# A fused convolution and two-layer network on Trainium2: weight conversion, first convolutions and first pairs in an interleaved order, part of the conversion on DVE

## The chip, the cores and the metric

The kernel runs on one core of a Trainium2 chip. The metric is the device time of one execution in microseconds. Times of one kernel are medians of several runs; a trace comes from one more execution, which has its own time.

## The reference

What is computed, cut to its core: a causal convolution of width 7, whose weights are a softmax for each token and head, and after it two matrix products with a leaky ReLU between them.

```python
# x: (4, 4096, 192), weight_gen: (4, 4096, 8, 7), w_in: (192, 2048), w_out: (2048, 192)
w = np.exp(weight_gen - np.max(weight_gen, axis=-1, keepdims=True))
w = w / (np.sum(w, axis=-1, keepdims=True) + 1e-09)
x_unf = x_pad[:, idx, :].reshape(B, S, K, H, group)      # the 7 last tokens of each token
x = np.einsum('bshk,bskhg->bshg', w, x_unf).reshape(B * S, D)
h = x @ w_in
g = np.maximum(0.01 * h, h)
return g @ w_out
```

The two weight matrices arrive as 64-bit numbers (two 32-bit words each). All results are 32-bit.

## The kernel before, in words

The 16384 tokens are cut into 32 chunks `c` of 512. The hidden layer's 2048 columns are cut into 8 pairs of 2 x 128, so there are 32 x 8 = 256 steps `q`, each with one chunk and one pair. `step(q)` issues `mm1` (18 matmuls into two PSUM buffers `hp`, tag `h`, of which there are four), then `act` for both (ACT applies the ReLU in place and makes the upper half `gh`; DVE subtracts and makes the lower half `gl`), and `mm2` for an earlier pair (20 matmuls into `po`). Every 32-bit operand is split into an upper and a lower half of the matmul's number format, and products are summed from the halves.

The weights are converted on the chip while the first chunk runs. There are 16 pieces: 8 of `w_in` (`wi_raw`, one for each pair) and 8 of `w_out` (`wo_raw`). Each goes through five stages, named by letters:

- `r`: ACT reads the low and the high words (L108, L109);
- `w`: DVE joins them in three instructions (L119, L121, L125), the first two in a PSUM buffer of tag `h`, and SP then gets the load of a later piece;
- `o`: an integer addition rounds up (L133), on POOL; the capital `O` does it on DVE;
- `u`: the upper half is cast (L154), on ACT; the capital `U` does it on DVE (L152);
- `l`: the lower half is subtracted (L158), on POOL; the capital `L` does it on DVE.

The convolution of chunk 0 (L246 and L256: three quarters of it on DVE, letters `d` and `e`; a quarter on POOL, letter `g`) ends in `twice` (L251), which PE transposes (`T`, L275). Chunk 1's convolution is POOL's (13 instructions, letter `p`). Its result is split (`c`: ACT L287; `v`: POOL L291), transposed in blocks by DVE (`t`, `m`: L297, into `sq`) and spread by 16 transfers of SP's queue into `xx` (`x`, L310). Step 8, the first step of chunk 1, needs these transfers. Later chunks go the same way, fed to the queues by `step` itself.

The order in which all this is handed out up to step 9 is the string `START`, one letter for one piece of work; `s` is one call of `step`. There is no scheduler: each engine runs what it is handed in that order, and waits where an operand or a buffer isn't ready. After the string, the remaining steps are handed out one after the other.

Of the kernel before, what the change touches and what calls it, by code (L numbers as in the profile page):

```python
# [24 lines left out]

C0 = 1

START = "ASrdegdegdegdegdegdegdegwOuLdegdegdegdegdegdegrTppppsrwoulppppsrwoulrwoulppppsrwoulrwoulpsrwoulrwoulcsrwoulrwoulvtsrwoulrwoulmxsrwoulrwoulsrwoulwoulss"


@with_exitstack
def conv_attention_moe_kernel(
# [390 lines left out]
    with tc.manual_schedule():  # L423
# [81 lines left out]
        n = 0  # L505
        for what in START:
            if what in stages:
# [62 lines left out]
```

## Time and profile before

| | |
|---|---|
| median of 3 runs | 1249.89 us (1249.32 to 1250.35) |
| the profiled execution's own time | 1249.38 us |
| its span in the trace | 1247.6 us |
| PE busy (matmuls) | 1164.3 us, 93% of the span |
| ACT busy | 885.0 us, 71% |
| POOL busy | 810.0 us, 65% |
| DVE busy | 598.5 us, 48% |
| mean granted TensorE clock | 0.97 |

Times in the trace are counted from the span's start. The execution's time is 1.8 us more than the span, and 0.5 us less than the median. Busy shares are means over the whole span; the first 203 us, in which the weights are converted and the first chunks are started, look different from the rest. Matmul ends are modelled, so a busy PE is read as "not waiting", not as PE at its peak.

### The profile page before, as it was taken

To read this page: it belongs to the slowest core of one execution; us is meant where nothing else is said; L and a number is where in the kernel's file an instruction comes from. 1 tells how busy PE (TensorE), PEld (TensorE's weight loads), DVE (VectorE), ACT (ScalarE), POOL (GpSimd) and SP (SyncE) were. 2 spreads that over 40 slices of the span, in tenths; PEclk is the share of its full clock that TensorE was granted. 3 is DMA by queue.
4 is the path that set the end of the run, shared out by engine and by line. 5 is a ranking of instruction groups with operands and counts; after the bars stand their busy time and mean duration, and the time that the engine had idled before them with its cause. 6 is when DMAs were issued, how large, how long until landed. Compare 5 with 4: busy or idle time off the path is not lost.

```text
span 1247.6 us, 24837 instructions
## 1 busy us (share of the span) xinstructions
PE 1164.3 (93%) x9740; PEld 989.1 (79%) x9740; DVE 598.5 (48%) x890; ACT 885.0 (71%) x1940; POOL 810.0 (65%) x535
## 2 busy tenths in 40 slices
PE   2567798999999999999999999999999999999997
PEld 1345676888888888888888888888888888888885
DVE  6345343544545444444545454544545444454443
ACT  2344664788777777878777777777777778877775
POOL 5845847777666667876666677766666677866400
PEclk9688988999999999999999999999999999999999
DMA  3424204242231324233231424223232424221220
GB/s 102 128 64 115 45 21 116 64 115 65 52 104 43 98 65 116 64 98 70 55 99 44 112 65 116 64 63 102 48 94 55 116 65 116 65 52 45 49 49 26
DMA packets 118306, 94.93 MB, mean 76 GB/s; under 512 B 9391, under 2 KB 111791, under 8 KB 116398
## 3 DMA queue, kind: packets, MB, share of 16 engines
q1 hardware_dynamic: 116110, 92.18, 29.1%
q10 hardware_dynamic: 2080, 1.18, 0.4%
q8 instruction: 76, 1.25, 0.4%
q14 instruction: 40, 0.33, 0.1%
HBM read 31.98 MB, written 12.58 MB: 36 GB/s over the span
## 4 chain that ended last, share of the span: by engine, by line
PE 89%; DVE 3%; ACT 2%; SPq 2%; POOL 1%; issue 1%; ACTq 1%; DMA 1%; DVEq 0%; POOLq 0%
PE po L357 46%; PE hp L329 43%; SPq L310 2%; ACT hp L336 1%; POOL bits L133 1%; ACTq L310 1%; ACT gh L338 0%; DVE gl L340 0%; DMA xx<-sq 0%; DVE h L246 0%; ACT wi_h L154 0%; DVE t L121 0%; DVE bits L125 0%; DVE sq L297 0%; POOL acc L256 0%
## 5 line engine op out<-in xcount | busy, mean ns | idle before, releaser
L329 PE MATMUL hp<-xx,wi_h 64*128 64x512 f32 x3072 | 583.2, 402 | 53.0 <-ACT wi_h L154 26.7
L340 DVE TENSOR_TENSOR gl<-hp,gh 128x512 fp32r<-128x512 f32 x512 | 353.4, 690 | 580.7 <-ACT gh L338 579.4
L357 PE MATMUL po<-gh,wo 64*128 64x512 f32 x3072 | 628.8, 393 | 0.0
L357 PE MATMUL po<-gl,wo 64*128 64x512 f32 x2048 | 547.9, 392 | 0.0
L329 PEld LDWEIGHTS hp<-xx,wi_h 64*128 64x128 f32 x3072 | 439.7, 189 | 111.0 <-ACT wi_h L154 36.4
L357 PEld LDWEIGHTS po<-gh,wo 64*128 64x128 f32 x3072 | 477.1, 185 | 51.8
L329 PE MATMUL hp<-xx,wi_l 64*128 64x512 f32 x1536 | 471.1, 401 | 0.1
L336 ACT ACTIVATE hp<-hp 128x512 f32<-128x512 f32 x512 | 299.9, 586 | 208.7 <-PE hp L329 208.7
L357 PEld LDWEIGHTS po<-gl,wo 64*128 64x128 f32 x2048 | 372.8, 184 | 34.2
L256 POOL TENSOR_TENSOR acc<-acc,tmp 128x768 f32<-128x768 f32 (+1 forms) x191 | 346.3, 1813 | 14.7
L338 ACT CAST gh<-hp 128x512 fp32r<-128x512 f32 x512 | 300.4, 587 | 16.2
L329 PEld LDWEIGHTS hp<-xx,wi_l 64*128 64x128 f32 x1536 | 283.1, 189 | 30.7 <-POOL wi_l L158 4.3
L246 POOL TENSOR_TENSOR tmp<-xt,wt 128x768 f32<-128x768 f32 (+1 forms) x192 | 291.4, 1518 | 12.5
L395 ACT COPY ot<-z 32x128 f32<-32x128 f32 x752 | 223.3, 297 | 11.6 <-DVE z L379 0.9
L291 POOL TENSOR_TENSOR split<-acc,split 128x768 fp32r<-128x768 f32 x31 | 57.5, 1854 | 184.6 <-ACT split L287 184.6
L370 ACT COPY sa<-po 128x512 f32<-128x512 f32 x64 | 37.5, 586 | 59.5 <-PE po L357 59.5
L209 POOL TENSOR_TENSOR wt<-wt,mx 128x448 f32<-128x448 f32 x15 | 14.6, 975 | 99.0 <-DVE mx L206 96.4
L371 DVE TENSOR_TENSOR sa<-po,sa 128x512 f32<-128x512 f32 x64 | 43.0, 672 | 45.5 <-ACT sa L370 45.5
L297 DVE STREAM_TRANSPOSE sq<-split 128x768 f32<-128x768 f32 x62 | 56.8, 953 | 0.0
L246 POOL TENSOR_TENSOR acc<-xt,wt 128x768 f32<-128x768 f32 (+1 forms) x32 | 48.9, 1528 | 0.1
L395 POOL COPY ot<-z 32x128 f32<-32x128 f32 x8 | 2.7, 332 | 62.0 <-DVE z L379 61.7
L133 POOL TENSOR_TENSOR bits<-bits,rnd 128x384 uint32<-128x384 uint32 x15 | 15.0, 997 | 27.3 <-DVE bits L125 27.3
(47 smaller groups left out, 265.4 us busy)
## 6 DMA issues: line engine op xcount, KB each, us to landing
xx<-sq SPq DMA_DIRECT2D x488, 96.0 KB, 2.3
xt<-in_x_dram SPq DMA_DIRECT2D x14, 1344.0 KB, 6.5
out_dram<-ot SPq DMA_DIRECT2D x32, 384.0 KB, 2.5
wt<-in_weight_gen_dram SPq DMA_DIRECT2D x16, 224.0 KB, 3.1
wo_raw<-in_moe_w_out_dram SPq DMA_DIRECT2D x8, 384.0 KB, 3.6
wi_raw<-in_moe_w_in_dram SPq DMA_DIRECT2D x14, 192.0 KB, 3.4
xt<-in_x_dram SPq DMA_DIRECT2D x1, 960.0 KB, 5.1
xx<-sq ACTq DMA_DIRECT2D x8, 96.0 KB, 3.9
```

Of the source, the lines that this page charges most:

```text
L246: eng.tensor_tensor(out=ov, in0=xv, in1=wk, op=ALU.mult)
L256: eng.tensor_tensor(out=acc, in0=acc, in1=out, op=ALU.add)
L291: eng.tensor_tensor(out=l, in0=att.pop(c), in1=h.bitcast(F32), op=ALU.subtract)
L297: nc.vector.transpose(out=sq[c][:, i], in_=split[c][:, i].bitcast(F32).rearrange("p j (b d) -> p b j d", d=BK),)
L329: nc.tensor.matmul(out=hp[2 * q + u], lhsT=w[s], rhs=r[s], start=(m == 0), stop=(m == len(passes) - 1),)
L336: nc.scalar.activation(out=t, in_=t, func=AF.Prelu, alpha=0.01)
L338: nc.scalar.copy(out=g_h[n], in_=t)
L340: nc.vector.tensor_tensor(out=g_l[n], in0=t, in1=g_h[n].bitcast(F32), op=ALU.subtract)
L357: nc.tensor.matmul(out=po[which, u], lhsT=wo[s, f, w], rhs=g[n][s], start=(f == 0 and m == 0), stop=(f == NF - 1 and m == len(passes) - 1),)
L370: nc.scalar.copy(out=a, in_=po[which, 0])
L371: nc.vector.tensor_tensor(out=a, in0=po[which, 1], in1=a, op=ALU.add)
L395: engs[n % len(engs)](out=ot[k * BK:(k + 1) * BK, :, a * BK:(a + 1) * BK], in_=src[:, k])
```

## The change

Only the string `START` is another one. The pieces of work are the same, with the same letters in another order; six of the 16 integer additions (`o`) have become `O` and run on DVE (one did before), five of the 16 lower halves (`l`) have become `L` (one before), and four of the 16 casts (`u`) have become `U` (none before).

```diff
-START = "ASrdegdegdegdegdegdegdegwOuLdegdegdegdegdegdegrTppppsrwoulppppsrwoulrwoulppppsrwoulrwoulpsrwoulrwoulcsrwoulrwoulvtsrwoulrwoulmxsrwoulrwoulsrwoulwoulss"
+START = "ASdeegdegddegddeeeeddegpggrgwgdgeOgdrepggeeduprgldpdwopTwurwpsLorwrpopurOulupplwsLwOprsOurlwpwuorsouurlwlOrwlurwlswprooucLouwtUvmosrLwrUlswoUOlxUlsLss"
```

How ACT's queue stands around the first step, before. The first row is the last ReLU of step 0, the last row the first one of step 1; `rnd` and `mag` are the low and the high words of a piece, `wi_h` is its upper half.

```order
L336 ACTIVATE hp<-hp 128x512
L338 CAST gh<-hp 128x512
L108 ACTIVATE rnd<-wi_raw 128x384
L109 ACTIVATE mag<-wi_raw 128x384
L154 CAST wi_h<-bits 128x3x128
L336 ACTIVATE hp<-hp 128x512
```

ACT's queue now, from the end of the first transposes (`xx<-ta`) to the first ReLU of step 0.

```order
L280 CAST xx<-ta 128x512 x3
L154 CAST wi_h<-bits 128x3x128
L108 ACTIVATE rnd<-wo_raw 128x384
L109 ACTIVATE mag<-wo_raw 128x384
L336 ACTIVATE hp<-hp 128x512
L338 CAST gh<-hp 128x512
```

The cast that step 1's `mm1` needs stood behind step 0's ReLUs and behind the reading of its own piece; now it stands ahead of step 0's ReLUs, and so does the reading of later pieces.

DVE's queue from step 1's lower halves `gl` to step 2's, before; `t` and `bits` are the three instructions that join a piece's words.

```order
L340 TENSOR_TENSOR gl<-hp,gh 128x512 x2
L119 TENSOR_SCALAR t<-mag 128x384
L121 TENSOR_SCALAR t<-t 128x384
L125 SCALAR_TENSOR_TENSOR bits<-wi_raw,t 128x384
L119 TENSOR_SCALAR t<-mag 128x384
L121 TENSOR_SCALAR t<-t 128x384
L125 SCALAR_TENSOR_TENSOR bits<-wo_raw,t 128x384
L340 TENSOR_TENSOR gl<-hp,gh 128x512 x2
```

The same stretch now; `L133 ISA` is the integer addition on DVE.

```order
L340 TENSOR_TENSOR gl<-hp,gh 128x512 x2
L158 TENSOR_TENSOR wi_l<-bits,wi_h 128x3x128
L119 TENSOR_SCALAR t<-mag 128x384
L121 TENSOR_SCALAR t<-t 128x384
L125 SCALAR_TENSOR_TENSOR bits<-wi_raw,t 128x384
L133 ISA bits<-bits,rnd 128x768
L340 TENSOR_TENSOR gl<-hp,gh 128x512 x2
L133 ISA bits<-bits,rnd 128x768
```

The piece joined here belongs to a later step than before: by the `gl` that opens the stretch, DVE has joined six pieces, against two before. Additions and lower halves stand between.

SP's queue, the one piece in which it differs.

```order
 L98 DMA wo_raw<-in_moe_w_out_dram 128x2x384
 L95 DMA wi_raw<-in_moe_w_in_dram 64x3x256 x2
-L176 DMA wt<-in_weight_gen_dram 128x448
-L184 DMA xt<-in_x_dram 128x2688
 L98 DMA wo_raw<-in_moe_w_out_dram 128x2x384
 L95 DMA wi_raw<-in_moe_w_in_dram 64x3x256 x2
 L98 DMA wo_raw<-in_moe_w_out_dram 128x2x384
+L176 DMA wt<-in_weight_gen_dram 128x448
+L184 DMA xt<-in_x_dram 128x2688
```

The loads for chunks 2 and 3 (`wt`, `xt`) stand behind two more pieces of weights than before. The 16 transfers into `xx` still stand behind the last load of `wo_raw`. PE's queue is the same instruction for instruction.

## Rows read from the trace of the kernel before

**Rows 1.** --windows: stretch, length, busy us of PE, PEld, DVE, ACT, POOL, PEclk

```profile
21.00:112.10 91.10, 52.78 (x277) 36.85 (x278) 41.15 (x72) 40.56 (x79) 49.41 (x49) 0.75 0.32 88
112.10:159.20 47.10, 37.97 (x306) 31.14 (x306) 18.48 (x26) 27.75 (x61) 41.89 (x29) 0.90 0.28 75
159.20:203.20 44.00, 38.23 (x306) 32.15 (x306) 17.26 (x25) 26.66 (x59) 25.47 (x17) 0.93 0.20 43
203.20:1241.00 1037.80, 1035.31 (x8855) 888.95 (x8855) 502.95 (x722) 784.69 (x1730) 678.01 (x416) 1.00 0.30 75
```

**Rows 2.** Chain that ended last, over step 5 (start, us, what)

```profile
77.98 3.90 PE hp L329 x16
81.88 2.35 PE po L357 x20
...
84.25 0.69 DVE gl L340
84.94 0.48 DVE t L119
...
86.73 1.00 POOL bits L133
...
88.32 0.79 PE hp L329
```

**Rows 3.** DVE's groups from 0 to 112 us, shapes apart (--lines)

```profile
L340 DVE TENSOR_TENSOR gl<-hp,gh 128x512 fp32r<-128x512 f32 x16 | 11.1, 692 | 39.8 <-ACT gh L338 39.0 <-PE po L357 0.8
L121 DVE TENSOR_SCALAR t<-t 128x384 uint32<-128x384 uint32 x16 | 9.1, 566 | 0.6
L119 DVE TENSOR_SCALAR t<-mag 128x384 f32<-128x384 f32 x16 | 8.8, 551 | 0.0
L125 DVE SCALAR_TENSOR_TENSOR bits<-wo_raw,t 128x384 uint32<-128x384 uint32 x8 | 4.4, 554 | 0.7
...
L281 DVE TENSOR_TENSOR xx<-ta,xx 128x512 fp32r<-128x512 f32 x3 | 2.1, 692 | 1.7 <-ACT xx L280 1.7
L297 DVE STREAM_TRANSPOSE sq<-split 128x768 f32<-128x768 f32 x2 | 1.9, 972 | 0.0
...
L158 DVE TENSOR_TENSOR wi_l<-bits,wi_h 128x384 fp32r<-128x384 f32 x1 | 0.9, 891 | 0.6 <-ACT wi_h L154 0.6
L133 DVE CUSTOM_DVE_ANT_0 bits<-bits,rnd 128x768 uint16<-128x768 uint16 x1 | 0.8, 843 | 0.0
```

**Rows 4.** Timelines of PE, DVE and SP at six places

```profile
21.12 2.83 PE L275 MATMUL ta<-ident,twice 128*128 128x128 f32 x12 [21.12 <-DVE twice L251]
...
44.70 1.22 PE L329 MATMUL hp<-xx,wi_h 64*128 64x512 f32 x4 [6.39 <-DVE bits L125]
...
84.25 0.69 DVE L340 TENSOR_TENSOR gl<-hp,gh 128x512 fp32r<-128x512 f32 x1 [0.41 <-PE po L357]
...
88.28 0.97 DVE L297 STREAM_TRANSPOSE sq<-split 128x768 f32<-128x768 f32 x1
...
99.69 10.52 SPq L310 DMA_DIRECT2D xx<-sq  x16
...
112.10 1.19 PE L329 MATMUL hp<-xx,wi_h 64*128 64x512 f32 x3 [0.87 <-DMA xx<-sq]
```

**Rows 5.** Busy time around step 8's start, columns as in rows 1

```profile
111.83:115.24 3.41, 3.14 (x15) 2.70 (x17) 0.00 (x0) 0.51 (x1) 2.79 (x6) 0.50 1.00 376
115.24:118.65 3.41, 3.41 (x32) 2.96 (x30) 1.32 (x2) 2.24 (x4) 3.33 (x4) 1.00 0.20 85
```

**Rows 6.** Two lines of DVE (--source: min/median/max ns), and one meeting with POOL (timeline)

```profile
L218 DVE TENSOR_SCALAR sm<-sm x16: 195/1196/1242, 6.0 to 1093.1; 128x64 f32<-128x64 f32 x16
...
L376 DVE TENSOR_TENSOR sb<-sa x32: 685/686/2079, 122.2 to 1240.1; 64x512 f32<-64x512 f32 x32
...
241.11 1.84 POOL L256 TENSOR_TENSOR acc<-acc,tmp 128x768 f32<-128x768 f32 x1
...
241.86 1.15 DVE L218 TENSOR_SCALAR sm<-sm 128x64 f32<-128x64 f32 x1
```

## The prediction

> **What bounds the kernel now.** I read the busy time by stretch first. From 203.2 us on, PE is busy 1035.3 of 1037.8 us at the full clock, 2.4 GHz; the reader is to see that there is nothing to win there, since the change leaves PE's queue and all later work as they are [rows 1]. From 21.0 to 112.1 us, the eight steps of chunk 0, PE is busy 52.8 of 91.1 us at a mean granted clock of 0.75, and no engine is full: DVE 41.2, ACT 40.6, POOL 49.4 us [rows 1]. When all wait, the bound is a chain, so I read the chain of waits over one step next [rows 2]. Step 5 starts at 77.98 and step 6 at 88.32, a loop of 10.34 us through every engine: PE 3.90 for `mm1`, 2.35 for `mm2`, with the ReLUs beside it; DVE's lower half at 84.25; only then the join of the next weights at 84.94 (DVE), the addition at 86.73 (POOL), the cast (ACT), and PE again. The weights of a step are begun after the step ahead of it has gone through ACT and DVE. From 84.25 to 88.32 PE has nothing to do. The same shows on DVE: 39.8 us of idle time stand before 16 `gl` [rows 3].
>
> Third, the end of this stretch. Step 8 waits for the transfers into `xx`. The block transposes that feed them end at 88.28 + 0.97 = 89.25, but SP issues them from 99.69, 10.4 us later, and PE starts at 112.10 [rows 4]. The last loads of `w_out` stand ahead of them in SP's queue and need a raw buffer that DVE frees with its 14th join; before the second transpose it has done 12.
>
> **What the change removes.** ACT's and DVE's orders show it: casts and joins of later pieces now stand ahead of a step's ReLUs and lower halves. The loop of rows 2 is cut, because when `mm1` of a step ends, the next weights are under way or done. PE's own work bounds a step then, or the queue of an engine. PE: 8 x 18 + 6 x 20 = 264 matmuls ahead of step 8. At 2.4 GHz it takes 3.41/32 = 0.107 us for one, at 1.2 GHz 3.41/15 = 0.227 [rows 5]; that is 28 to 60 us from about 25, so PE could be at step 8 between 53 and 85.
>
> **DVE's queue sets the new time.** Six additions, five lower halves and four casts go there, so I count it. PE's first transpose waits for DVE until 21.1 [rows 4]. In the new order the same work stands ahead of that, less one lower half that goes to POOL (0.89 and its wait of 0.6 [rows 3]); POOL's quarter gets three instructions of chunk 1 between its own and may end later. So between 19.6 and 21.1; I take 20.8. From there to the end of the second block transpose DVE has, in the order printed, with durations from rows 3:
> 13 joins of 0.551 + 0.566 + 0.554 = 1.67: 21.7; 10 `gl` of 0.692: 6.9; 4 additions of 0.843: 3.4; 3 lower halves of 0.891: 2.7; 3 `xx` of 0.692: 2.1; 2 transposes of 0.972: 1.9; one maximum, 0.6 (an estimate from the 0.55 of a join's instruction); one cast, which DVE does not do before: between the 0.195 of the small `sm` [rows 6] and the 0.692 of a larger subtraction, 0.5. Together 39.8 us.
> Waits that stay: 1.7 before the `xx` [rows 3]; 0.4 between the two `gl` of each of 5 steps, as at 84.25 [rows 4], 2.0; gaps inside a join, 86.73 - 84.94 - 1.67 = 0.12 [rows 2, 3], 13 times, 1.6. Together 5.3 us.
> 20.8 + 39.8 + 5.3 = 65.9 for the end of the transposes, against 89.25. The 14th join now stands ahead of the transposes, so the last load leaves SP in time and the transfers follow at once. From their first issue to PE it is 112.10 - 99.69 = 12.4 [rows 4]: step 8 at 78.3. That is 33.8 us earlier, and PE, with its 53 to 85, is there in time if it gets more than a quarter of its stretch at the high clock.
>
> POOL does not bind: of its 49.4 busy us in this stretch [rows 1] five additions and four lower halves go to DVE, and what is left ahead of chunk 1's split fits into the 45 us from 20.8 to 65.9.
>
> **The clock.** Before step 8 PE had been idle; its first stretch, 111.83 to 115.24, was granted 0.50 and got 15 matmuls done where the next one did 32 at 1.00 [rows 5]. That cost 3.41 x (1 - 15/32) = 1.8 us. With PE busy up to 78 and only a short gap, I count it as saved; the other end is nothing saved.
>
> **After step 8** the same instructions follow: 47.1 us to step 16 and 44.0 to step 24 [rows 1], both held by chunk 2's and chunk 3's convolution, split and transfers, which start with the steps. POOL is busy 41.9 of those 47.1 us, so it must begin chunk 2 no later against step 8 than now. Its leftover additions are fewer, so I price this at nothing; if that cover is gone, each late us is lost once. The loads of `wt` and `xt`, two pieces later in SP's queue, are needed at step 8 and have tens of us. Their cost is nothing too.
>
> Sum, against the profiled execution's 1249.38: 33.8 + 1.8 = 35.6, so 1213.8. The median of the runs is 0.5 above that execution: 1214.3.
>
> **A cost that speaks against it.** Line 218, a small DVE instruction between SBUF tensors, takes 0.195 us alone and 1.196 in the median; at 241.86 it ran 1.15 us and ended 0.06 after POOL's addition of 241.11. Line 376, which reads two SBUF tensors, takes 0.686, and once 2.079 [rows 6]. So such instructions of DVE wait for the POOL instruction under way. All 15 added ones read and write SBUF alone. The Trainium skill says so as a rule, in SBUF — State Buffer, section "SBUF: two separate sides": the port pair of the two engines is "an exclusive lock, not a bandwidth split", and the later one blocks for a whole instruction. The trace agrees with it (1.15 against 0.195). By that rule alone, with each of the eight added or kept ahead of the second transpose behind a full POOL addition of 1.84, 14.7 us would go and 1229 be left. I keep the measured durations, since the one addition and the one lower half that DVE has now (0.843, 0.891) ran while POOL was working; the larger waits are the first rival.
>
> **Rivals.**
> 1. *DVE waits for POOL.* Line 376's worst wait is 2.079 - 0.686 = 1.39. For the eight ahead of the second transpose that is 11.1 us, and 1225.4; for all 15, if the later ones hold PE too, 20.9, and 1235. For it: POOL is busy over half of the time. Against it: most meetings will be with shorter instructions or their ends. From 1226 to 1238, 0.10.
> 2. *The order changes nothing.* If each step's cast still came after the ReLUs, through another wait, the loop of 10.34 us would stay, and 1250. Against it: the printed orders of ACT and DVE. 0.02.
> 3. *The four buffers of tag `h` close a longer loop.* A join takes one, `mm1` two. At 44.70 PE was let go by a join of `w_out`, not by its weights [rows 4]: so it has waited for a buffer. If every `mm1` waited for the `gl` of the step before and then for two joins, an addition and a lower half queued behind it, a step would take 3.90 + (84.94 - 81.88) + 2 x 1.79 + 0.84 + 0.89 = 12.3, against 10.34. Eight steps make 15 us, and 1265. It decides from the point where more than one join and its addition stand between a `gl` and the next `mm1`. In the stretch printed there are one of each and one lower half, and 2.35 us of `mm2` run beside them. 0.03.
> 4. *Better.* With no wait for ACT between `gl`, 19.6 as the start and 2 x 1.8 of low clock saved at steps 16 and 24 as well, 33.8 + 2.0 + 1.2 + 1.8 + 3.6 = 42.4, and 1207. Below 1206: 0.01.
>
> **Numbers.** The forecast, 1206 to 1226, has 0.84: its low end is rival 4's 1207, its high end the eight waits of rival 1 at 1225. The likeliest time is the sum, 1214.3. Faster by over 0.2% (2.5 us, about what a measurement of this kernel can tell from no change): 0.84 + 0.10 + 0.01 = 0.95. Within 0.2%: rival 2, 0.02. Slower: rival 3, 0.03.
>
> **What would show it.** In the changed kernel's profile: steps 0 to 7 some 6 to 7 us apart, not 10.3; no idle time of PE before step 2 to 7 that ACT's `wi_h` ends; the second transpose ending near 66 and SP's 16 transfers right behind it; step 8's first matmuls near 78; then 47 and 44 us to steps 16 and 24, and the same from there. DVE's idle time before `gl` up to step 8 should fall from 39.8 to below 10. Wrong would be: additions on DVE of over 1.5 us in the mean (rival 1), or `mm1` released by `gl` and L125 in every step with 10 us between steps (rival 3), or a step 16 more than 48 us behind step 8 (POOL).

## The result and the profile after

The changed kernel takes 1214.49 us in the median of four runs (1211.91 to 1217.24), the kernel before, beside it on the same chip, 1250.12 (1249.32 to 1250.64). The ratio is 0.9716, with an interval of 0.9689 to 0.9743: 35.6 us less. The profiled execution of the changed kernel took 1211.91 us, the fastest of its four; its span is 1210.1 us, its mean granted clock 0.985.

Busy time by stretch of the changed kernel, with the columns of [rows 1] and cut at the same steps: 8, 16 and 24. The last row is the part of the first one in which DVE works from PE's first transpose to its own second block transpose.

```profile
21.00:75.72 54.72, 44.05 (x277) 31.90 (x278) 48.25 (x85) 37.75 (x74) 42.97 (x40) 0.88 0.54 147
75.72:121.64 45.92, 36.45 (x306) 34.63 (x306) 19.73 (x29) 27.25 (x60) 40.62 (x25) 0.94 0.29 77
121.64:165.70 44.06, 38.54 (x304) 32.30 (x304) 16.97 (x25) 26.66 (x59) 24.88 (x17) 0.93 0.19 42
165.70:1203.50 1037.80, 1035.63 (x8855) 859.74 (x8855) 502.71 (x721) 784.74 (x1729) 678.07 (x416) 1.00 0.30 75
...
21.01:62.63 41.62, 32.93 (x201) 23.49 (x201) 37.59 (x64) 31.80 (x63) 38.42 (x35) 0.88 0.50 149
```

The first stretch, with the same 277 matmuls, is 36.4 us shorter (91.10 before). The second lost 1.2 us, the third nothing, and the 1037.8 us behind them are as they were. In the first stretch DVE is now busy 48.25 of 54.72 us, and in the part of it in the last row DVE 37.59 and POOL 38.42 of 41.62 us: two engines are nearly full, where before the fullest, PE and POOL, were busy for 58 and 54% of the stretch.

The chain of waits of the changed kernel over step 4 (start, length, what), to lay beside [rows 2]:

```profile
48.58 0.48 DVE t L119
...
49.74 0.57 DVE bits L125
...
50.35 3.18 PE hp L329 x16
...
53.55 0.59 ACT hp L336
...
55.89 0.69 DVE gl L340
56.59 0.48 DVE t L119
```

The join at 49.74 is no longer that of the next step's weights: PE goes on when it ends because the join's buffer of tag `h` comes free. POOL and the cast are gone from the chain; it stays on DVE.

The timeline of the changed kernel, with rows of PE, DVE and SP (start, length, engine, line, operation):

```profile
50.35 0.74 PE L329 MATMUL hp<-xx,wi_h 64*128 64x512 f32 x3 [1.22 <-DVE bits L125]
...
56.21 1.16 PE L329 MATMUL hp<-xx,wi_h 64*128 64x512 f32 x4
...
57.74 0.56 DVE L125 SCALAR_TENSOR_TENSOR bits<-wi_raw,t 128x384 uint32<-128x384 uint32 x1
58.21 0.55 DVE L158 TENSOR_TENSOR wi_l<-bits,wi_h 128x384 fp32r<-128x384 f32 x1
...
61.67 0.96 DVE L297 STREAM_TRANSPOSE sq<-split 128x768 f32<-128x768 f32 x1
...
62.66 11.16 SPq L310 DMA_DIRECT2D xx<-sq  x16
...
75.72 0.69 PE L329 MATMUL hp<-xx,wi_h 64*128 64x512 f32 x3 [0.90 <-DMA xx<-sq]
...
119.11 0.76 PE L329 MATMUL hp<-xx,wi_h 64*128 64x512 f32 x1 [7.70 <-DMA xx<-sq]
121.64 1.19 PE L329 MATMUL hp<-xx,wi_h 64*128 64x512 f32 x3 [1.76 <-DMA xx<-sq]
```

Step 5 starts at 56.21 with no wait ahead of it, while step 4's last `gl` (55.89) is still running: the loop of 10.34 us is cut. The second block transpose ends at 62.63, and SP's 16 transfers begin 0.03 us later, where 10.4 us stood between them before [rows 4]. Step 8 starts 13.06 us after the first of them. The next places that wait stand at the bottom: step 16 waits 7.70 and 1.76 us for its transfers.

DVE's groups from 0 to 76 us, with the columns of [rows 3]:

```profile
L340 DVE TENSOR_TENSOR gl<-hp,gh 128x512 fp32r<-128x512 f32 x16 | 10.8, 686 | 4.2 <-ACT gh L338 4.1
...
L133 DVE CUSTOM_DVE_ANT_0 bits<-bits,rnd 128x768 uint16<-128x768 uint16 x6 | 5.3, 888 | 0.1
...
L158 DVE TENSOR_TENSOR wi_l<-bits,wi_h 128x384 fp32r<-128x384 f32 x3 | 2.6, 856 | 0.0
L281 DVE TENSOR_TENSOR xx<-ta,xx 128x512 fp32r<-128x512 f32 x3 | 2.1, 691 | 0.6 <-ACT xx L280 0.6
```

The idle time before the 16 `gl` fell from 39.8 to 4.2 us. That these 35.6 us are also the kernel's gain is chance: up to step 8 all idle time of DVE fell from 49.95 to 6.47 us, its busy time grew by 7.10, and the difference is the 36.4 us.

### The profile page after: what moved, and what is told of

It reads as the page before. It is cut to its first block, busy times and chain, and to the rows that moved or that the text cites. A ratio compares the mean times of both kernels' runs of the same rounds, so it can differ in the third digit from the quotient of the medians.

```text
span 1210.1 us, 24837 instructions
## 1 busy us (share of the span) xinstructions
PE 1154.7 (95%) x9740; PEld 958.6 (79%) x9740; DVE 607.1 (50%) x905; ACT 883.1 (73%) x1936; POOL 802.3 (66%) x524
## 4 chain that ended last, share of the span: by engine, by line
PE 91%; DVE 3%; SPq 2%; DMA 1%; ACT 1%; issue 1%; POOL 0%; ACTq 0%; DVEq 0%
PE po L357 47%; PE hp L329 43%; SPq L310 2%; DMA xx<-sq 1%; ACT hp L336 1%; DVE sq L297 0%; DVE h L246 0%; DVE gl L340 0%; ACT gh L338 0%; DVE acc L256 0%; DVE t L121 0%; DVE bits L125 0%; DVE t L119 0%; PE ta L275 0%; DMA wt<-in_weight_gen_dram 0%
## 5 line engine op out<-in xcount | busy, mean ns | idle before, releaser
L357 PE MATMUL po<-gl,wo 64*128 64x512 f32 x2048 | 554.4, 392 | 0.0
L329 PEld LDWEIGHTS hp<-xx,wi_h 64*128 64x128 f32 x3072 | 435.0, 186 | 91.4 <-issue 15.4
L329 PE MATMUL hp<-xx,wi_l 64*128 64x512 f32 x1536 | 476.2, 396 | 0.0
L357 PEld LDWEIGHTS po<-gl,wo 64*128 64x128 f32 x2048 | 377.9, 185 | 39.7
L209 POOL TENSOR_TENSOR wt<-wt,mx 128x448 f32<-128x448 f32 x15 | 14.7, 977 | 99.2 <-DVE mx L206 96.6
L222 POOL TENSOR_TENSOR wt<-wt,sm 128x448 f32<-128x448 f32 (+1 forms) x16 | 15.3, 959 | 19.4 <-DVE sm L219 19.4
```

Source lines behind the costliest of these rows:

```text
L329: nc.tensor.matmul(out=hp[2 * q + u], lhsT=w[s], rhs=r[s], start=(m == 0), stop=(m == len(passes) - 1),)
L357: nc.tensor.matmul(out=po[which, u], lhsT=wo[s, f, w], rhs=g[n][s], start=(f == 0 and m == 0), stop=(f == NF - 1 and m == len(passes) - 1),)
```

## The experiments

The theory: the order of the pieces does it, by cutting the loop and by freeing SP's queue; which engine does an addition, a half or a cast hardly counts. The first rival: moving the work to DVE does it, because POOL's and ACT's parts of the loop get shorter. The second: SP's queue does it, and more raw buffers would give most of it in the old order. A third question came later: is it the lead of the weights over the steps, or the places in between?

**The new order, engines as before.** The letters stand as in the change, but all that became a capital is small again (one `O` and one `L` remain, as before the change).

```diff
-...eduprgldpdwopTwurwpsLorwrpopurOulupplwsLwOprsOurlwpwuorsouurlwlOrwl...
+...eduprgLdpdwopTwurwpslorwrpopuroulupplwslwoprsourlwpwuorsouurlwlorwl...
```

> The new order, with the additions, lower halves and casts on the engines that had them before (one addition and one lower half on DVE). First theory, the order cuts the loop of one step: nearly all of the gain stays. POOL gets back five additions of 0.99 us and four lower halves of about 1 us, which can delay chunk 1's split by a few us: step 8 at 76 to 82 instead of 75.7, time 1214 to 1221. Second theory, the gain is DVE's relief of POOL: the nine us of POOL's work come back in every loop, step 8 not before 90, time over 1228.

Measured: 1215.11 us (1213.82 to 1215.87), ratio 0.9713 [0.9699, 0.9728]. The timeline of this kernel:

```profile
66.11 11.17 SPq L310 DMA_DIRECT2D xx<-sq  x16
...
79.22 0.70 PE L329 MATMUL hp<-xx,wi_h 64*128 64x512 f32 x3 [0.50 <-DMA xx<-sq]
```

And its busy time from PE's first transpose to DVE's second block transpose, columns as in [rows 1]:

```profile
22.02:66.08 44.06, 33.72 (x201) 23.74 (x201) 32.00 (x56) 31.26 (x63) 41.48 (x40) 0.92 0.48 144
```

The order alone gives the gain. With eight pieces of work less on DVE in this stretch, DVE is busy for 32.00 us and no longer full, but POOL now is, with 41.48 of 44.06. SP's transfers begin 3.5 us later here than in the profile of the changed kernel, but other executions with the changed string begin them as late (below), and the changed kernel, timed beside it, took 1214.08: 1.0 us less, with ranges that overlap. So no gain of the moved instructions was measured.

**The engines alone, in the old order.** The same pieces' additions, halves and casts go to DVE; no letter changes its place.

```diff
-START = "...rTppppsrwoulppppsrwoulrwoulppppsrwoulrwoulpsrwoul...srwoulrwoulsrwoulwoulss"
+START = "...rTppppsrwouLppppsrwoulrwoulppppsrwOuLrwOulpsrwOul...srwoUlrwoUlsrwoUlwOULss"
```

> The old order, with the same pieces' additions, lower halves and casts on DVE as in the change. First theory: the loop through PE, ACT, DVE, and addition stays, so steps stay about 10 us apart; an addition on DVE saves 0.99 + 0.14 against 0.84 in three or four steps, some 2 to 4 us in all: 1245 to 1249. Second theory: at least a third of the gain, 12 us or more: under 1238.

Measured: 1250.66 us (1248.45 to 1251.61, ten runs), ratio 0.9997 [0.9988, 1.0007]: no change; the expected 2 to 4 us less did not come. Its timeline at step 5:

```profile
87.32 1.22 PE L329 MATMUL hp<-xx,wi_h 64*128 64x512 f32 x4 [4.12 <-ACT wi_h L154]
```

PE still waits 4.12 us for the cast of the step's weights; the loop is there. Taking an instruction out of POOL's part of the loop puts it into DVE's part of the same loop. The first rival falls.

**Four raw buffers for `w_out` instead of two, in the old order.**

```diff
-            w = raw.tile([P, 2, D, 2], U32, tag="wo", name="wo_raw")
+            w = raw.tile([P, 2, D, 2], U32, tag="wo", name="wo_raw", bufs=4)
```

> The kernel before with four raw buffers of w_out instead of two, so that the last loads don't wait for DVE's 14th join and SP can issue the 16 transfers of chunk 1 when the transposes end, near 89. If the prediction's reading of SP's queue is right, the transfers land near 102, and step 8 waits for PE's own step 7, which ends near 106.6, instead of 112.1: 5 to 7 us gained, 1243 to 1245. If the transfers were late for another reason (DVE, or the transfers' own length), step 8 stays at 112 and the time at 1250.

Measured: 1247.6 us (1245.95 to 1249.2, ten runs), ratio 0.9977 [0.9968, 0.9986]: 2.4 us less, under half of the expected 5 to 7. The timeline of this kernel at step 8:

```profile
89.54 11.57 SPq L310 DMA_DIRECT2D xx<-sq  x16
...
105.86 0.73 PE L329 MATMUL hp<-xx,wi_h 64*128 64x512 f32 x3 [0.55 <-DVE gl L340]
...
110.53 0.50 PE L357 MATMUL po<-gh,wo 64*128 64x512 f32 x2 [2.30 <-ACT wo L154]
```

The transfers now follow the transposes (89.54, where they began at 99.69 [rows 4]), and step 8 starts over 6 us earlier. Then `mm2` waits for the last pieces of `w_out`, which the old order converts late, and most of it is given back: step 9 starts 2.8 us earlier (117.40 against 120.16). So SP's queue was a second lock, as read, but worth little before the first one is open.

**The changed kernel once more**, unchanged, beside the last three.

> The changed kernel once more, since its four times lie 5.3 us apart (1211.9 to 1217.2) where those of before lie within 1.3. If the granted clock's low stretches at the starts of steps 0 to 24 fall differently in each execution, a second profile has the same order of waits with step 8, 16 and 24 some us later or earlier, and low stretches of another length. If something else differs (transfers, the port), durations of DVE or transfers differ instead.

Measured: 1214.08 us (1212.49 to 1215.08), ratio 0.9705 [0.9691, 0.9719]. Its profiled execution took 1213.46 us, and it parts from the other one at step 0. First the changed kernel's first profile, timeline of DVE and one row of POOL:

```profile
28.60 0.69 DVE L340 TENSOR_TENSOR gl<-hp,gh 128x512 fp32r<-128x512 f32 x1
...
30.32 0.80 DVE L158 TENSOR_TENSOR wi_l<-bits,wi_h 128x384 fp32r<-128x384 f32 x1
...
32.81 1.09 DVE L133 CUSTOM_DVE_ANT_0 bits<-bits,rnd 128x768 uint16<-128x768 uint16 x1
...
37.35 1.21 DVE L158 TENSOR_TENSOR wi_l<-bits,wi_h 128x384 fp32r<-128x384 f32 x1
...
31.95 1.54 POOL L246 TENSOR_TENSOR tmp<-xt,wt 128x768 f32<-128x768 f32 x1
```

The same instructions in the second profile, and two rows of POOL:

```profile
30.11 0.69 DVE L340 TENSOR_TENSOR gl<-hp,gh 128x512 fp32r<-128x512 f32 x1 [1.67 <-ACT gh L338]
...
31.82 1.63 DVE L158 TENSOR_TENSOR wi_l<-bits,wi_h 128x384 fp32r<-128x384 f32 x1
...
35.15 1.50 DVE L133 CUSTOM_DVE_ANT_0 bits<-bits,rnd 128x768 uint16<-128x768 uint16 x1
...
40.04 2.23 DVE L158 TENSOR_TENSOR wi_l<-bits,wi_h 128x384 fp32r<-128x384 f32 x1
...
31.49 1.55 POOL L246 TENSOR_TENSOR tmp<-xt,wt 128x768 f32<-128x768 f32 x1
...
40.04 1.82 POOL L256 TENSOR_TENSOR acc<-acc,tmp 128x768 f32<-128x768 f32 x1
```

Busy time of PE from 24.20 to 27.60 us, where step 0 begins, in the first profile, columns as in [rows 1]:

```profile
24.20:27.60 3.40, 2.85 (x18) 1.78 (x18) 3.14 (x7) 1.87 (x5) 3.32 (x3) 1.00 0.80 227
```

And in the second:

```profile
24.20:27.60 3.40, 3.28 (x13) 2.31 (x15) 3.14 (x7) 1.58 (x4) 3.32 (x3) 1.00 0.79 224
```

PE got 18 matmuls done there in one execution and 13 in the other; the granted clock reads 1.00 in both rows, so why PE was slower stays open. The first `gl` comes 1.5 us later, DVE's next instructions fall on other instructions of POOL, and the same two halves and the addition take 5.36 instead of 3.10 us. Three of these six end 0.41 us after the POOL instruction shown beside them: 33.90 after 33.49, 33.45 after 33.04, 42.27 after 41.86. As these ends read, DVE waited for POOL's instruction to end, and did its own work then. In the four later kernels with this string (below) PE also got 13 done there, and SP's transfers begin between 64.68 and 66.40; here they begin at 64.65. The first profile, with 62.66, was the favourable one. The two profiled executions lie 1.6 us apart (1211.91 and 1213.46), under a third of the 5.3 us between the changed kernel's four runs; no trace of a run at 1217 is there to show the rest. Nor is it settled which of the two theories holds: DVE's durations differ, but from 34.40 to 37.80 us the granted clock differs too, 0.95 in the first profile and 0.50 in the second.

**The old order, one step ahead.** Every group of the old string (read, join, add, cast, halve) stands whole, but behind the step before the one it stood behind; engines as before.

```diff
-START = "...rTppppsrwoulppppsrwoulrwoulppppsrwoulrwoulpsrwoulrwoulcsrwoulrwoulvt..."
+START = "...rTpppprwoulspppprwoulrwoulspppprwoulrwoulsprwoulrwoulscrwoulrwoulsvt..."
```

> The old order with each group of weight work (read, join, addition, cast, lower half) moved one step ahead, as a block; nothing else is moved. Theory a: it is enough that a step's weights are ready when its mm1 comes; steps 6 to 7 us apart and 1214 to 1222. Theory b: the blocks still tie ACT, since a step's ReLUs stand behind casts that wait for the join and the addition behind the lower halves of the step before; a loop of 3 (ReLUs and lower halves) + 1.8 (join) + 1.0 (addition) + 0.5 (cast), and part of a second join, addition and cast, stays without mm1 in it; steps 8 to 9.5 us apart, 1232 to 1243. Then the interleaving inside a group is needed, not only the lead.

Measured: 1238.38 us (1237.47 to 1239.43), ratio 0.9905 [0.9888, 0.9922]: 12 us of the 36. The timeline of ACT in this kernel:

```profile
37.59 0.51 ACT L154 CAST wi_h<-bits 128x384 fp32r<-128x384 f32 x1 [5.88 <-POOL bits L133]
...
74.13 0.55 ACT L109 ACTIVATE mag<-wo_raw 128x384 f32<-128x384 f32 x1
78.19 0.51 ACT L154 CAST wi_h<-bits 128x384 fp32r<-128x384 f32 x1 [3.52 <-POOL bits L133]
...
80.80 0.51 ACT L154 CAST wo<-bits 128x384 fp32r<-128x384 f32 x1 [1.20 <-POOL bits L133]
81.22 0.58 ACT L336 ACTIVATE hp<-hp 128x512 f32<-128x512 f32 x1
```

The weights lead by a step, and still the ReLU at 81.22 stands behind two casts which wait 3.52 and 1.20 us for the join and the addition of pieces that no one needs yet. In a queue that runs in order an early instruction whose operand isn't ready holds all that is behind it: ACT's idle time before the 15 casts that follow its first one is 41.2 us here, 32.6 in the kernel before and 7.9 in the new order with engines as before. So the lead alone isn't enough.

This edit has a second effect, though. Two groups now stand behind a block of four convolution instructions in POOL's queue, and their casts wait 5.88 us (37.59) and 6.96 us (50.74) for POOL. The ReLUs of steps 1 and 2 come 12.1 and 13.1 us after those of the step before (10.9 and 10.8 in the kernel before); those of steps 3 to 5, where no such block stands, 8.9, 8.9 and 9.8 us (11.9, 10.4 and 10.3). What the lead alone gives without such blocks was not tried.

**The casts a step behind the joins.** As the last one, but each group is cut in two: read, join and add behind one step, cast and halve behind the next.

```diff
-START = "...rTppppsrwoulppppsrwoulrwoulppppsrwoulrwoulpsrwoulrwoulcsrwoulrwoulvt..."
+START = "...rTpppprwoulrwosppppulrworwosppppululrworwospululrworwoscululrworwosvt..."
```

> The old order in blocks, engines as before, but each group is cut in two: read, join and addition of two pieces behind one step, their casts and lower halves behind the next step, where the additions are long done. So ACT's queue holds no cast that waits for a join between two steps' ReLUs. If the block of ACT by such casts is what keeps the 9 to 10 us of a step when the group is only moved ahead whole, steps come to 7 to 8 us and the time to 1214 to 1226. If the interleaving with the convolutions is what matters, steps stay at 9 us or more: over 1232.

Measured: 1222.82 us (1222.3 to 1223.18), ratio 0.9785 [0.9768, 0.9801]: 27 of the 36 us, with the engines as before and in plain blocks. The timeline of ACT, and a row of PE:

```profile
51.47 0.51 ACT L154 CAST wo<-bits 128x384 fp32r<-128x384 f32 x1 [5.84 <-POOL bits L133]
...
57.87 0.51 ACT L154 CAST wo<-bits 128x384 fp32r<-128x384 f32 x1
58.28 0.51 ACT L154 CAST wi_h<-bits 128x384 fp32r<-128x384 f32 x1
...
49.15 0.79 PE L357 MATMUL po<-gh,wo 64*128 64x512 f32 x2 [5.01 <-POOL wo L158]
```

Most of ACT's casts no longer wait, as the two at 57.87 and 58.28: the idle time before these 15 is 10.9 us, and 5.84 of them stand before the one at 51.47. What is left shows there and in the last row, where `mm2` waits 5.01 us for a lower half of POOL. Ahead of that half, and of the addition that the cast waits for, four convolution instructions of chunk 1 stand in POOL's queue from 41.46 on, a block of four letters `p`. The change spreads these letters. That this accounts for all of the other 9 us was not tried by itself.

Nor do the 15 us between this run and the last one belong to the casts alone. The joins lead further here, 15 ahead of the second block transpose instead of 12, and so SP's queue is open: its transfers begin 0.03 us behind that transpose (at 73.35), where they began 3.8 us behind it in the last run (88.97 after 85.13).

**Chunk 2's split one step earlier.** From here on the start is the changed one, and the next place in line is moved: the step behind which a chunk's split and transposes are handed out.

```diff
-                m = i - {1: 5, 2: 4, 3: 2}.get(c, 1)
+                m = i - {1: 4, 2: 4, 3: 2}.get(c, 1)
```

> The changed kernel, with chunk 2's split (ACT L287, POOL L291) and what follows it one step earlier in chunk 1 (after step 12 instead of 13). If chunk 2's transfers set step 16 and start with the steps, step 16 comes up to 3 us earlier, as POOL ends chunk 2's convolution near 100 and the split then waits for that: 1211 to 1214. If POOL's convolution or the transfers on ACT's queue hold it, no change: 1214 to 1215.

Measured: 1211.17 us (1208.34 to 1211.73), ratio 0.9681 [0.9666, 0.9695]. PE at step 16 in this kernel:

```profile
119.18 0.76 PE L329 MATMUL hp<-xx,wi_h 64*128 64x512 f32 x1 [3.52 <-DVE gl L340]
```

The wait of 7.70 us is 3.52 now and has another cause: `gl`, whose ReLU stands on ACT behind ACT's own eight transfer issues (109.16 to 117.13).

**Chunk 3's split two steps earlier.**

```diff
+                m = i - {1: 5, 2: 2, 3: 2}.get(c, 1)
```

> The changed kernel, with chunk 3's split two steps earlier in chunk 2 (after step 18 instead of 20). POOL has ended chunk 3's convolution long before. If the split's place sets step 24, its transfers land before step 23 ends, the gap of 5.4 + 1.3 us ahead of step 24 and the low clock behind it (6.8 us at 1.2 GHz, about 3 us of work) go: 7 to 9 us less, 1205 to 1208. If chunk 4's convolution, which the same number starts earlier, delays POOL's lower half or a later chunk, less than 3 us: over 1211.

Measured: 1205.34 us (1203.68 to 1208.64), ratio 0.9642 [0.9624, 0.966]. Busy time of this kernel from step 16 to step 24:

```profile
126.88:164.50 37.62, 37.62 (x304) 31.35 (x306) 16.17 (x24) 26.51 (x59) 25.85 (x17) 0.93 0.25 54
```

PE is busy all of the 37.62 us; the stretch took 44.06 before this edit. Its wait ahead of step 24 is gone. The profiled execution is the slowest of the four (1208.64): its step 16 came 5.2 us later than in the changed kernel's first profile.

**Both.**

```diff
+                m = i - {1: 4, 2: 2, 3: 2}.get(c, 1)
```

> The last two together: the sum of both if they are independent, 1202 to 1208.

Measured: 1200.57 us (1197.29 to 1200.7), ratio 0.9594 [0.9579, 0.9609], the best of all and below the expected range: 13.9 us less than the changed kernel, where the two edits gave 3.3 and 9.2 by themselves. Why they give more together was not looked for. The timeline of ACT and of PE at step 16 in this kernel:

```profile
107.70 7.85 ACTq L310 DMA_DIRECT2D xx<-sq  x8
115.60 0.58 ACT L336 ACTIVATE hp<-hp 128x512 f32<-128x512 f32 x1 [9.36 <-DMA xx<-sq]
...
117.63 0.76 PE L329 MATMUL hp<-xx,wi_h 64*128 64x512 f32 x1 [3.95 <-DVE gl L340]
```

**Both, and chunk 2's transfers all on SP's queue**, to take the eight issues from ACT:

```diff
-                        spread_squares(c + 1, [nc.sync, nc.scalar] if c == 1 else [nc.sync])
+                        spread_squares(c + 1, [nc.sync])
```

> The changed kernel with both splits earlier, and chunk 2's 16 transfers all on SP's queue instead of half on ACT's. If ACT's 7.9 us of issuing, which hold back step 14's ReLUs, are what PE waits for ahead of step 16, the gap of 4.3 us shrinks and PE does steps 14 and 15 meanwhile: 1198 to 1201. If the transfers themselves are the bound, 16 on one queue land 12.4 us after the transposes, near 120, and step 16 comes 1 to 2 us later than with both queues: 1201 to 1204.

Measured: 1200.94 us (1200.05 to 1205.1), ratio 0.9617 [0.96, 0.9634]: no better. PE at step 16 in this kernel:

```profile
122.09 0.76 PE L329 MATMUL hp<-xx,wi_h 64*128 64x512 f32 x1 [5.01 <-DMA xx<-sq]
```

ACT is free, but 16 issues in one queue take 10.81 us, and now the transfers end last. That is read from the slowest of the four executions (1205.1); the median lies at the border of the two expected ranges and doesn't decide between them.

## Why the prediction was right

| step of the prediction | predicted | changed kernel's profile |
|---|---|---|
| steps 0 to 8, one from the next | 6 to 7 us | (75.72 - 24.35) / 8 = 6.4 us |
| idle time of DVE before `gl` | below 10 us | 4.2 us |
| first transpose of PE | 20.8 | 21.01 |
| end of the second block transpose | 65.9 | 62.63 |
| first transfer issue to step 8 | 12.4 us | 13.06 us |
| step 8 | 78.3 | 75.72 |
| low clock after step 8 | 1.8 us less | 8 to 16: 47.1 to 45.92, 1.2 us less |
| steps 16 to 24, and from there on | no change | 44.0 to 44.06; no change |
| sum in the span | 35.6 us less | 36.4 + 1.2 - 0.1 = 37.5 us less |

**The loop** fell as read: the step spacing, `gl` and the chain all show it, and the kernel with the engines alone, which keeps the old order, keeps the loop and its time.

**DVE's queue** set the time in the changed kernel, whose chain over step 4 stays on it, and its count was exact: the instructions counted are those that ran. Their durations, by the groups of this stretch, add up to 39.7 us, where the prediction had 39.8; but the stretch has only 37.59 us of busy time: an instruction that doesn't need the one before begins some 0.1 us before that one ends (58.21 against 57.74 + 0.56). Adding durations counts these laps twice, some 2 us here. The waits are 41.62 - 37.59 = 4.0 us, not 5.3: the three `xx` wait 0.6, not 1.7. This term was 3.3 us too late, against this favourable profile; the other executions, at 64.65 to 66.40, lie on both sides of 65.9.

DVE is not the only bound, however. The prediction held that POOL does not bind, and POOL is busy 38.42 of these 41.62 us, as full as DVE. With eight pieces taken off DVE (the new order, engines as before) POOL was the full one, and the transposes ended at 66.08, no earlier than here. So the two queues are about even, and moving work between them gained nothing here. Of the 15 instructions that the prediction calls added, 13 are new on DVE (five additions, four lower halves, four casts); one addition and one lower half ran there before. The sum above counts only what stands in the stretch and isn't touched; rival 1's 20.9 us would be 18.1.

**SP's queue**: the claim that the 14th join frees it ahead of the transposes holds to 0.03 us. The transfers cost 0.7 more than counted, as their 16 issues took 11.16, not 10.52 us.

**The clock**: 1.8 us were counted as saved, and the stretch behind step 8 is 1.2 us shorter. From 75.72 to 79.13 the granted clock was 1.00 and PE got 30 matmuls done, where it was 0.50 with 15 before [rows 5]; but around step 16 it is still 0.50 (116.1 to 122.9 us now, 155.4 to 162.2 before).

**The rivals.** DVE does wait for POOL, and by the whole rest of an instruction, but an addition takes 0.888 us in the mean, not over 1.5. The Trainium skill's rule (SBUF — State Buffer, "SBUF: two separate sides") describes what the rows show, each time with the 0.41 us behind POOL's end; the 14.7 us that the rule alone would have cost did not come. The eight instructions ahead of the second transpose took 6.5 us in the first profile and 8.6 in the second; each at the shortest that its kind took (0.55, 0.55 and 0.51 us) they would take 4.4, so the waits cost 2.2 and 4.3 us. The buffers of tag `h` hold PE in places (1.22 us at 50.35), never for a loop. POOL began chunk 2 at 76.98, 1.3 us after step 8 (3.1 before), and was in time.

**The sum.** That the median came within 0.2 us of 1214.3 is partly luck. The span of the profiled execution shrank by 1.9 us more than forecast: DVE's term was 3.3 us too high, the transfers' 0.7 too low, and the clock's saving 0.6 too high. This execution was the fastest of the four.

What the prediction did not see: that the same order with the conversion left on POOL and ACT would do as well, and that a lead of one step would not. It named the lead as what cuts the loop. The runs show that whole groups a step ahead give 12 us, joins further ahead with the casts a step behind them 27, and the interleaved order 36. How these parts divide between the casts' places, SP's queue and POOL's blocks was not tried apart.

## What to carry to other kernels

When no engine is full, follow the chain over one turn of the loop and ask of each in-order queue which instruction stands ahead of the one that is needed. An instruction that prepares later work belongs where its operand has long been ready: early issue with a late operand holds everything behind it. After such a place is opened, read the profile again; the next wait had been hidden, and moving two splits, one number each, gave another 14 us (1214.49 to 1200.57).

## What was unexpected in the hardware

The same program had two forms of its first 40 us. They part in how many matmuls PE does in its first 3.4 us at step 0, 18 or 13, and after a shift of 1.5 us DVE's waits for POOL were 2.3 us longer. A cost that depends on which two instructions meet isn't a constant: the same lower half took 1.21 us in one execution and 2.23 in the other. And POOL is held in turn: beside DVE's addition of 32.81, its own half took 1.31 us (start 33.45), where its shortest took 0.99.
